# Another written order for the whole instruction list of a Mamba-2 and low-rank mixer kernel

## The chip, the cores and the metric

The kernel runs on one core of a Trainium2 chip. Its engines are TensorE (PE, the matrix products; PEld is its loading of weights), VectorE (DVE), ScalarE (ACT), GpSimd (POOL) and SyncE (SP, whose queue issues the DMAs). The metric is the time of one execution on the device in microseconds, the median of several runs. The profile is of one execution; its span is counted from the first to the last recorded instruction.

## The reference

The input is x (4 batches, 8 heads, 768 steps, 32 channels), a decay a for each step, and B and C (16 states a step). All is float32, though U, V, w_ch1 and w_ch2 come as float64 words.

```python
for c in range(nc):                          # chunks of 32 steps
    cum = np.cumsum(la, axis=-1)             # la = log(clip(a))
    M = einsum('bhin,bhjn->bhij', Cc, Bc) * exp(cum_i - cum_j) * causal
    y = einsum('bhij,bhjd->bhid', M, xc)                     # inside the chunk
    y += einsum('bhin,bhnd->bhid', Cc, state) * exp(cum)     # from before it
    state = decay_full * state + sum_j(Bc * xc * exp(cum_last - cum))
# y of all heads side by side: X of (4, 768, 256)
u = X + (X^T @ U @ V)^T                      # U: 768 x 32, V: 32 x 768
out = u + relu(u @ w_ch1) @ w_ch2            # 256 -> 1024 -> 256
```

## The kernel before

The first half (the scan) takes the steps in 12 **pairs** of two 128-step blocks, three pairs a batch: pairs 0 to 2 are batch 0, and so on. The second half (the mixer) takes each batch in two halves of 384 steps, with the 1024 inner channels in 8 groups.

**The order.** Nothing schedules these instructions: the text PLAN is a list of words, and `follow` (L886) goes through it and emits the instructions of each word, so each engine gets its instructions in the order of the words. An engine works its own list in order and waits at the first instruction that lacks its input. A shorter text, LOADS, is gone through before PLAN and issues the first loads. The words, with k a pair, b a batch, j a half and m an inner group:

- **F**n: the next bank of PSUM that is taken is first written by n products that nobody reads (`idle`, L139). The number is set, not added to (`fills[0] = n`), so a later F ahead of the bank replaces it.
- **A**i: the decays. A0 is product L370, A1 the products L374; each is followed by an exponential on ACT (L377). The logarithm is L342. K: what each state keeps.
- **Q**k.c, **P**k: prep, B and C times the decays (DVE, tile BC). **V**, **T**: turning, the transposes of BC on PE (w, x or y) and their copies T and Cm (by ACT, or Cm by DVE).
- **g**k: gram (L507), 16 products for C times B. **m**k, **M**k: the causal mask, two banks each (DVE, tile M). **s**k, **u**k: state (L542) and its update (L569: four on DVE, one on POOL).
- **n**k, **j**k: the two halves of the product inside the chunk (`intra`, L652); j has to follow one DVE instruction that comes after n's products, and where no such one is at hand it adds a copy to `settled`. **i**k: `inter` (L627). **y**k: the copy out to yT (ACT). **t**k, **O**k: transposes back to steps (`ytokens`, L679).
- **B**k, **X**k, **w**n: loads of B and C, of x, and of weight blocks (SP, `begin`, L195). Each of these words holds its first DMA until the last DVE instruction emitted so far is done. SP issues in order, so what stands behind a held DMA stands too. **L**k: B and C and x of pair k, held in the same way. V0 and U0 in LOADS are the loads of V and U, not held.
- **c**c: one of three steps of the conversion of weight block c from float64 words to float32 (`to_fp32`, L417 and L422): two instructions on DVE and one on ACT; one on DVE; the addition on POOL. Block 0 is U and V; 1 to 5 are w_ch1 (w1f); 6 to 9 are w_ch2.
- **v**0: spread, V copied to the form that the mixer needs (copy L838, products L844, copies to Vs). **R**c: a step of splitting a weight block in rounded parts.
- **p**b, **q**b, **a**b.j: X^T @ U (L705), its parts (L713), and the product with V that DVE adds to yT (L723). **S**b.j: the split of u in three parts (ACT L746, then DVE), in one buffer with w1f.
- **U**b.j.m: in batch 0, four products of 128x384 in plain float32 and a relu. **f**, **e**, **h** b.j.m: elsewhere, u @ w_ch1 in four and two products of rounded parts, the relu on ACT (L785) after e, and a difference on DVE in h. **d**b.j.k.n: piece n of the product with w_ch2 for 128 steps; the last piece is followed by the sum on DVE and the output's DMA. The products of U, f, e and d all have line L751.

Two banks of PSUM stand behind each of the tags w, x, z and y; a bank is taken again when its last reader is done.

Of the kernel before, what the change touches and what calls it, by code (L numbers as in the profile page):

```python
# [10 lines left out]
FP32 = mybir.dt.float32  # L11
INT32 = mybir.dt.int32
UINT32 = mybir.dt.uint32
FP32R = mybir.dt.float32r
WCOLS = 512
NWORDS = 15
# [14 lines left out]

LOADS = (
    'B0 X0 B1 V0 U0 X1 B2 X2 B3 ')
PLAN = (
# [36 lines left out]


@with_exitstack
def kernel(
# [28 lines left out]
    P = 128  # L105
    NB, NH, S, D = x.shape
    N = B.shape[-1]
    NC = S // P
    NPR = NC // 2
    DM = NH * D  # L110
    RK = moe_U.shape[1]
# [6 lines left out]
    NQ = NM // 2  # L118
# [75 lines left out]
    def begin(**kwargs):  # L194
        op = nc.sync.dma_start(**kwargs)  # L195
        if until:
            hold(op, until.pop())

    def load_bc(k, blocks=(0, 1)):
        b, q = pairs[k]  # L200
        if k not in bc_sb:
            bc_sb[k] = raw.tile([P, NH, 2, 2, N], FP32, tag="bc", name="bc")
        for c in blocks:
            begin(
                out=bc_sb[k][:, :, 0, c],
                in_=B[b, :, ts(2 * q + c, P), :].rearrange("h s n -> s h n"))
            if c == 0:
                begin(
                    out=bc_sb[k][:, :, 1].rearrange("p h t n -> p h (t n)"),
                    in_=C[b, :, ts(q, 2 * P), :].rearrange("h (p t) n -> p h (t n)", t=2))  # L210
# [17 lines left out]
    w1all = mix.tile([P, NQ, NCB, W], FP32, tag="u", name="w1f", bufs=1)  # L228
    w1f = [w1all[:, c] for c in range(NQ)]
    w2 = [const.tile([P, NM, DM], FP32R, name=f"w2{i}") for i in range(2)]  # L230
    weights = []
    w2f, w2b = {}, {}

    def w2c(n, dtype):
        return (w2f if dtype == FP32 else w2b).setdefault(n, mix.tile(
            [P, 2, DM], dtype, tag=f"w2c{n}", name=f"w2c{n}", bufs=1))


    def words_of(dst):
        p, i, j = dst.shape  # L240
        t = raw.tile([P, 2 * WCOLS], INT32, tag="words", name="words", bufs=NWORDS)
        weights.append((dst, t[:p, :2 * i * j]))
        return t[:p, :2 * i * j]

    def each(parts, *index):
        return [part[index] for part in parts]

    def load_words(dst, src):

        p, i, j = dst.shape  # L250
        t = words_of(dst)
        begin(out=t.rearrange("p (i j) -> p i j", i=i), in_=src)

    U2, V2, w12, w22 = (w.bitcast(INT32) for w in (moe_U, moe_V, moe_w_ch1, moe_w_ch2))
# [3 lines left out]
    own = {}  # L258

    def load_v():  # L260
        own["UV"] = words_of(UV)
        for q in range(4):
            begin(out=own["UV"][ts(q, Q), 2 * NC * RK:], in_=V2[:, ts(q, 2 * NC * RK)])

    def load_u():
        begin(out=own["UV"][:, :2 * NC * RK].rearrange("p (c r) -> p c r", c=NC),
                          in_=U2.rearrange("(c p) r -> p c r", p=P))

    def load_w(n):
        if n < 2:  # L270
            if n == 0:
                own["w"] = words_of(w1f[0])
                weights.pop()
            dst, t = w1f[0][:, :, ts(n, P)], own["w"][:, ts(n, 2 * NCB * P)]
            weights.append((dst, t))
            begin(out=t.rearrange("p (i j) -> p i j", i=NCB),
                  in_=w13[:, :, ts(n, 2 * P)])
        elif n <= NQ:
            load_words(w1f[n - 1], w13[:, :, ts(n - 1, 2 * quarter)])
        else:  # L280
            m = 2 * (n - NQ - 1)
            load_words(w2c(n - NQ - 1, FP32), w22[m * P:(m + 2) * P].rearrange(
                "(m p) d -> p m d", p=P))

    def load(k):
        if k < NB * NPR:
            load_bc(k)
            load_x(k)

    loads = dict(B=load_bc, X=load_x, w=load_w)  # L290
    for word in LOADS.split():
        dict(loads, V=lambda n: load_v(), U=lambda n: load_u())[word[0]](int(word[1:]))

    ident = const.tile([P, P], FP32)
    make_identity(nc, ident)
# [578 lines left out]
    def ytokens_of(k, v):  # L874
# [1 line left out]

    scans = dict(P=prep, T=turned, g=gram, s=state, m=lambda k: mask(k, (0, 1)),
                 M=lambda k: mask(k, (2, 3)), u=update, i=inter, n=lambda k: intra(k, 0),
                 j=crossed, y=yout, t=ytokens, L=load, Q=lambda k, c: prep(k, c, 1),
                 O=ytokens_of,  # L880
                 V=lambda k, c, v: turn(k, c, 1, "wx"[v // 2], vector if v % 2 else None))
    whole = dict(c=convert, R=refined, A=lambda i: decays(every_batch, "w", [i]),
# [3 lines left out]
    def follow(plan):  # L886

        for word in plan.split():
            name, at = word[0], [int(v) for v in word[1:].split(".")]
            if name in "BXwL":  # L890
                until[:] = [vector.last]
            if name in loads:
                loads[name](*at)
            elif name in scans:
                scans[name](*at)
            elif name in whole:
                whole[name](*at)
            else:
                b, *at = at
                if b not in mx:  # L900
                    mx[b] = mixer(b)
                getattr(mx[b], name)(*at)
            until.clear()
# [32 lines left out]
```

## Time and profile before

| | |
|---|---|
| Median of 3 runs | 230.32 us (230.38, 229.53, 230.32) |
| Profiled execution | 229.32 us |
| its span | 227.6 us |
| granted TensorE clock, mean | 0.992 |
| PE busy | 215.0 us |
| DVE busy | 146.5 us |
| ACT busy | 107.9 us |
| POOL busy | 33.9 us |
| DMA | 14.56 MB, mean 64 GB/s |

The page cuts the span into 40 slices of some 5.7 us. Each digit is the busy share of a slice in tenths (9 is 90% or more); PEclk is the clock that TensorE was granted, in tenths of full speed; DMA is the busy share of the DMA engines:

```profile
PE   7867979999999999999999999999999999999993
PEld 5644636666658889887999897698999999999993
DVE  4597867678632686479746546967746964945731
ACT  2334643756854366532456511465445654636410
POOL 3031232335075003015200010000000000000000
PEclk9999988999999999999999999999999999999999
DMA  6896878976560164211430001000010000000011
```

The chain that ended last is followed back from the last instruction; its shares by engine, then by line:

```profile
PE 82%; DVE 10%; issue 2%; ACT 2%; POOL 1%; POOLq 0%; DVEq 0%
PE x L751 29%; PE z L751 20%; PE y L751 12%; PE y L652 3%; PE y L627 3%; DVE M L169 3%; PE x L507 2%; PE w L679 2%; DVE words L169 2%; PE w L705 2%; DVE S L169 2%; PE w L475 2%; DVE BC L169 2%; PE w L542 1%; PE w L139 1%
```

All of DVE's instructions bear the line of the helper that records them, L169, so they are told apart by their tiles. A row of a timeline gives the start in us, the busy time, engine, line, operation, tiles, and the number of instructions drawn together; in square brackets stands how long the engine was idle before it, and what ended that.

### The profile page before, as it was taken

The numbers are of one execution on the slowest core, as the hardware profiler recorded it, in microseconds if no ns is written. First come the engines' busy times: TensorE is split into PE (matmuls) and PEld (weight loads), VectorE is DVE, ScalarE is ACT, GpSimd is POOL, SyncE is SP. The second block draws the span as 40 slices with busy tenths as digits, with TensorE's granted clock in tenths as the row PEclk, the third lists the DMA queues.
The fourth block names the chain that finished last, engine by engine and source line by source line (L and its number), as shares of the span: only waits on it lengthen the run. The fifth ranks groups of instructions, "written<-read, shape, count | busy, mean of one in ns | idle before, by whom it ended". The sixth has DMA issues, their size and how long they took to land.

```text
span 227.6 us, 6973 instructions
## 1 busy us (share of the span) xinstructions
PE 215.0 (94%) x3004; PEld 183.3 (81%) x3004; DVE 146.5 (64%) x312; ACT 107.9 (47%) x250; POOL 33.9 (15%) x43
## 2 busy tenths in 40 slices
PE   7867979999999999999999999999999999999993
PEld 5644636666658889887999897698999999999993
DVE  4597867678632686479746546967746964945731
ACT  2334643756854366532456511465445654636410
POOL 3031232335075003015200010000000000000000
PEclk9999988999999999999999999999999999999999
DMA  6896878976560164211430001000010000000011
GB/s 95 137 130 111 154 180 162 232 106 202 80 94 23 35 106 49 42 32 50 53 65 27 22 27 49 3 3 0 3 46 3 24 0 26 23 23 26 23 46 46
DMA packets 69518, 14.56 MB, mean 64 GB/s; under 512 B 63792, under 2 KB 67696, under 8 KB 69488
## 3 DMA queue, kind: packets, MB, share of 16 engines
q1 hardware_dynamic: 69488, 14.13, 31.5%
q8 instruction: 23, 0.38, 0.6%
q14 instruction: 7, 0.06, 0.1%
HBM read 10.98 MB, written 3.15 MB: 62 GB/s over the span
## 4 chain that ended last, share of the span: by engine, by line
PE 82%; DVE 10%; issue 2%; ACT 2%; POOL 1%; POOLq 0%; DVEq 0%
PE x L751 29%; PE z L751 20%; PE y L751 12%; PE y L652 3%; PE y L627 3%; DVE M L169 3%; PE x L507 2%; PE w L679 2%; DVE words L169 2%; PE w L705 2%; DVE S L169 2%; PE w L475 2%; DVE BC L169 2%; PE w L542 1%; PE w L139 1%
## 5 line engine op out<-in xcount | busy, mean ns | idle before, releaser
L751 PE MATMUL x<-u,w 128*128 128x384 f32 x144 | 33.3, 345 | 0.1
L751 PE MATMUL z<-u,w 128*128 128x384 f32 x144 | 33.0, 344 | 0.0
L169 DVE SCALAR_TENSOR_TENSOR words<-words 128x768 fp32r<-128x768 f32 (+3 forms) x34 | 29.7, 873 | 2.1 <-PE y L751 0.4
L751 PEld LDWEIGHTS x<-u,w 128*128 128x128 f32 x144 | 24.5, 188 | 1.1 <-ACT words L785 0.4
L751 PEld LDWEIGHTS z<-u,w 128*128 128x128 f32 x144 | 24.8, 188 | 0.3
L169 DVE SCALAR_TENSOR_TENSOR words<-x,words 128x384 fp32r<-128x384 f32 x24 | 13.2, 555 | 17.7 <-ACT words L785 17.5
L756 ACT ACTIVATE x<-x 128x384 f32<-128x384 f32 (+1 forms) x30 | 13.7, 455 | 21.8 <-PE x L751 19.6
L751 PE MATMUL x<-w2c,words 128*128 128x256 f32 x112 | 22.4, 338 | 0.0
L756 ACT ACTIVATE z<-z 128x384 f32<-128x384 f32 (+1 forms) x27 | 12.5, 464 | 15.3 <-PE z L751 14.4
L569 POOL TENSOR_TENSOR Sm<-S,own 128x256 f32<-128x256 f32 (+1 forms) x12 | 7.7, 640 | 78.6 <-DVE S L169 60.1
L751 PEld LDWEIGHTS x<-w2c,words 128*128 128x128 f32 x112 | 18.3, 189 | 1.4
L751 PE MATMUL y<-w,words 128*128 128x256 f32 x144 | 19.3, 282 | 0.0
L751 PEld LDWEIGHTS y<-w,words 128*128 128x128 f32 x144 | 18.6, 190 | 0.0
L169 DVE SCALAR_TENSOR_TENSOR words<-z,words 128x384 fp32r<-128x384 f32 x24 | 13.2, 552 | 2.6 <-ACT words L785 2.6
L785 ACT ACTIVATE words<-x 128x384 fp32r<-128x384 f32 x24 | 11.7, 493 | 6.8 <-PE x L751 6.8
L785 ACT ACTIVATE words<-z 128x384 fp32r<-128x384 f32 x24 | 11.7, 491 | 6.7 <-PE z L751 6.7
L169 DVE TENSOR_TENSOR BC<-bc,F 128x512 f32<-128x512 f32 (+2 forms) x18 | 10.4, 594 | 5.5 <-ACT F L377 2.8
L507 PE MATMUL x<-Cm,T 32*64 32x128 f32 x192 | 11.0, 306 | 2.5 <-issue 1.4
L652 PE MATMUL y<-M,x 64*32 64x64 f32 x768 | 12.0, 223 | 1.5 <-DVE settled L169 1.5
L751 PE MATMUL x<-w,words 128*128 128x256 f32 x96 | 13.4, 284 | 0.0
L652 PEld LDWEIGHTS y<-M,x 64*32 64x32 f32 x768 | 8.2, 105 | 6.0 <-DVE settled L169 2.7
L751 PEld LDWEIGHTS x<-w,words 128*128 128x128 f32 x96 | 12.6, 190 | 0.1
(148 smaller groups left out, 406.4 us busy)
## 6 DMA issues: line engine op xcount, KB each, us to landing
words<-in_moe_w_ch_dram SPq DMA_DIRECT2D x7, 512.0 KB, 5.6
x<-in_x_dram SPq DMA_DIRECT2D x24, 128.0 KB, 3.4
out_dram<-ytok SPq DMA_DIRECT2D x24, 128.0 KB, 1.7
bc<-in_B_dram SPq DMA_DIRECT2D x24, 64.0 KB, 3.0
bc<-in_C_dram SPq DMA_DIRECT2D x12, 128.0 KB, 3.1
words<-in_moe_w_ch_dram SPq DMA_DIRECT2D x2, 256.0 KB, 3.2
words<-in_moe_V_dram SPq DMA_DIRECT2D x4, 48.0 KB, 2.0
words<-in_moe_U_dram SPq DMA_DIRECT2D x1, 192.0 KB, 3.0
```

Of the source, the lines that this page charges most:

```text
L139: nc.tensor.matmul(out=t[:, :m * w].rearrange("p (m i) -> p m i", i=w), lhsT=ident, rhs=ident[:, None, :w].to_broadcast([P, m, w]), start= ...
L169: self.last = call(*args, **kwargs)
L475: nc.tensor.transpose(out=tp[:, i, v], in_=s["BC"][:, i, c + v].rearrange("p h n -> p (h n)"), identity=ident)
L507: nc.tensor.matmul(out=g[r][cols, c], lhsT=s["T"][rows, 0, c, cols], rhs=s["Cm"][rows, :, :, ts(2 * c + p, Q)].rearrange("r v t i -> r v i ...
L569: nc.gpsimd.tensor_tensor(out=s["Sm"][:, sl], in0=s["S"][:, sl].rearrange("p i (s d) -> p i s d", s=2), in1=own2[:, b, 4 * q + sl.start:4 ...
L627: behind["first"].append(nc.tensor.matmul(out=y[r // 2][ts(r % 2, H), c, p], lhsT=own[ts(r, Q)], rhs=s["T"][ts(r, Q), 1, :, ts(2 * c + p, ...
L652: product = nc.tensor.matmul(out=y[n][ts(i, Q), c, p], lhsT=x_sb[k][half, c, h], rhs=s["M"][half, h // 2, c, h % 2], start=fresh(k, n, [i] ...
L679: nc.tensor.transpose(out=t[:, c, g], in_=yT[b][:, g, ts(2 * q + c, P)], identity=ident)
L705: nc.tensor.matmul(out=p[ts(c % 4, Q)], lhsT=U_sb[:, c], rhs=ytok[b][:, c], start=c < 4, stop=True, skip_group_check=True)
L751: nc.tensor.matmul(out=t, lhsT=lhsT, rhs=rhs, start=start, stop=True, skip_group_check=True)
L756: nc.scalar.activation(t, t, AF.Copy, scale=1.0 + EPS)
L785: nc.scalar.activation(gs[j, m // 2][0][:, m % 2], t, AF.Relu, scale=NEAR)
```

## The change

The two texts LOADS and PLAN become one PLAN with another order. The operations are those of before, save the fills: three products (F2 and F1) in place of five F words whose numbers add up to 13. The first loads stand in the list as words with a Y ahead (YB0, YX0, YV0, YU0), and are not held. L words are gone; their loads are B and X words. Weight blocks are kept by number, so that they can be loaded in any order.

The beginning of the list, before and after:

```diff
-LOADS = (
-    'B0 X0 B1 V0 U0 X1 B2 X2 B3 ')
 PLAN = (
-    'F5 A0 Q0.0 F1 F2 F4 w0 Q0.1 A1 Q0.2 V0.0.0 Q1.0 V0.1.1 K0 s0 Q1.2 g0 m0 Q1.1 M0 V1.0.2 '
-    'V1.1.2 u0 n0 g1 c0 c0 c0 M1 F1 i0 Q2.0 s1 j0 y0 m1 Q2.2 Q2.1 V2.0.2 u1 V2.1.3 n1 i1 g2 j1 y1 '
-    'B5 s2 m2 M2 w1 v0 u2 O0.0 w2 w3 c1 c1 c1 i2 P3 n2 j2 y2 t1 X3 T3 T3 B4 c2 c2 P5 O2.1 p0 g3 '
-    'c3 c3 w4 w5 m3 q0 M3 T5 w6 T5 a0.1 a0.0 s3 X4 c4 c4 c2 P4 U0.1.0 c5 c3 U0.0.3 U0.0.0 U0.0.2 '
-    'c4 c5 B6 X5 U0.1.1 T4 T4 U0.0.4 u3 n3 c6 i3 R2 g4 s4 j3 R1 M4 R0 c5 X6 m4 u4 U0.0.7 P6 c6 '
+    'F2 YB0 A0 Q0.0 A1 F1 YB1 Q0.1 Q0.2 V0.0.0 Q1.0 V0.1.1 Q1.1 K0 Q1.2 g0 m0 YX0 s0 M0 V1.1.2 '
+    'V1.0.2 n0 YB2 g1 YX1 w0 u0 Q2.2 i0 Q2.1 Q2.0 V2.0.2 m1 s1 j0 y0 M1 u1 V2.1.3 c1 n1 i1 g2 YV0 '
+    'YU0 c0 YX2 w1 j1 s2 y1 YB3 c0 c0 B5 m2 M2 X3 v0 u2 c2 c2 c2 O0.0 t1 i2 w2 B4 n2 j2 y2 P3 T3 T3 '
+    'c1 c1 R0 O2.1 p0 g3 P5 m3 q0 M3 T5 T5 a0.1 w4 X4 n3 s3 u3 X5 w3 U0.1.1 w6 B6 c3 P4 a0.0 U0.1.0 '
+    'i3 w5 c3 c5 c5 w8 T4 T4 w7 U0.0.0 c3 R1 U0.0.1 U0.0.2 U0.1.3 B11 j3 g4 B10 s4 y3 c5 U0.1.2 m4 '
```

Some places further on that differ (the whole list of the third and the fourth batch's words is reordered in the same manner):

```diff
-    'e1.1.2 h1.1.2 T10 e1.1.3 f1.1.4 f1.1.5 n8 i8 s10 j8 e1.1.4 e1.1.5 y8 d1.1.0.0 h1.1.3 '
+    'n8 h1.1.6 s10 j8 y8 h1.1.7 f1.1.3 u10 f1.1.4 e1.1.2 f1.1.5 h1.1.2 t7 T9 e1.1.4 h1.1.4 e1.1.3 '
+    'h1.1.3 e1.1.5 T9 d1.1.0.0 T10 d1.1.2.0 d1.1.1.0 d1.1.2.1 d1.1.2.2 d1.1.1.1 d1.1.0.1 h1.1.5 '
...
-    't8 g9 m9 p2 T11 i9 M9 q2 T11 g10 m10 n9 M10 a2.0 s11 j9 u11 y9 g11 m11 S2.0 M11 i10 t9 n10 '
+    'd1.1.1.5 t8 g9 T11 m9 M9 T11 p2 g10 m10 q2 M10 i9 n9 a2.0 s11 j9 y9 g11 m11 S2.0 n10 i10 '
...
-    'd2.0.0.0 h2.0.7 d2.0.1.0 d2.0.1.1 y11 a2.1 S2.1 d2.0.0.1 d2.0.0.2 d2.0.0.3 d2.0.1.2 d2.0.1.3 '
-    't10 t11 d2.0.1.4 d2.0.1.5 d2.0.0.4 d2.0.0.5 f2.1.1 f2.1.0 f2.1.2 f2.1.3 e2.1.0 h2.1.0 e2.1.1 '
+    'e2.0.3 j11 d2.0.0.0 h2.0.2 h2.0.3 d2.0.0.1 d2.0.1.0 d2.0.1.1 d2.0.1.2 S2.1 f2.1.0 d2.0.1.3 '
+    'd2.0.0.2 d2.0.0.3 d2.0.1.4 d2.0.1.5 e2.1.0 d2.0.0.4 d2.0.0.5 f2.1.1 h2.1.0 d2.0.2.0 y11 '
...
-    'd2.1.0.0 h2.1.6 a3.1 d2.1.0.1 d2.1.0.2 d2.1.2.1 d2.1.2.2 S3.0 f3.0.2 f3.0.3 f3.0.4 h2.1.7 '
+    'e2.1.6 h2.1.6 e2.1.7 S3.0 h2.1.7 d2.1.2.0 d2.1.2.1 d2.1.2.2 d2.1.0.1 d2.1.0.2 f3.0.2 f3.0.3 '
```

And the code around it:

```diff
-    weights = []
+    weights = {}
...
+    def both_words():
+        return weights[0][1] if 0 in weights else words_of(0, UV)
...
-            load_words(w1f[n - 1], w13[:, :, ts(n - 1, 2 * quarter)])
+            load_words(n + 1, w1f[n - 1], w13[:, :, ts(n - 1, 2 * quarter)])
...
-    for word in LOADS.split():
-        dict(loads, V=lambda n: load_v(), U=lambda n: load_u())[word[0]](int(word[1:]))
+    early = dict(loads, V=lambda n: load_v(), U=lambda n: load_u())
...
-            name, at = word[0], [int(v) for v in word[1:].split(".")]
-            if name in "BXwL":
+            name, rest = (word[:2], word[2:]) if word[0] == "Y" else (word[0], word[1:])
+            at = [int(v) for v in rest.split(".")]
+            if name in "BXw":
                 until[:] = [vector.last]
-            if name in loads:
+            if name[0] == "Y":
+                early[name[1]](*at)
+            elif name in loads:
```

More of the change, by code (lines that the diff above doesn't have):

```diff
@@ L236, in w2c, with words_of @@
             [P, 2, DM], dtype, tag=f"w2c{n}", name=f"w2c{n}", bufs=1))
-    def words_of(dst):
+    def words_of(c, dst):
         p, i, j = dst.shape
         t = raw.tile([P, 2 * WCOLS], INT32, tag="words", name="words", bufs=NWORDS)
-        weights.append((dst, t[:p, :2 * i * j]))
+        weights[c] = dst, t[:p, :2 * i * j]
         return t[:p, :2 * i * j]
@@ L246, in each, with load_words @@
         return [part[index] for part in parts]
-    def load_words(dst, src):
+    def load_words(c, dst, src):
         p, i, j = dst.shape
-        t = words_of(dst)
+        t = words_of(c, dst)
         begin(out=t.rearrange("p (i j) -> p i j", i=i), in_=src)
@@ L260, in load_v @@
     def load_v():
-        own["UV"] = words_of(UV)
+        t = both_words()
         for q in range(4):
-            begin(out=own["UV"][ts(q, Q), 2 * NC * RK:], in_=V2[:, ts(q, 2 * NC * RK)])
+            begin(out=t[ts(q, Q), 2 * NC * RK:], in_=V2[:, ts(q, 2 * NC * RK)])
+    def both_words():
+        return weights[0][1] if 0 in weights else words_of(0, UV)
     def load_u():
-        begin(out=own["UV"][:, :2 * NC * RK].rearrange("p (c r) -> p c r", c=NC),
+        begin(out=both_words()[:, :2 * NC * RK].rearrange("p (c r) -> p c r", c=NC),
                           in_=U2.rearrange("(c p) r -> p c r", p=P))
@@ L270, in load_w @@
         if n < 2:
-            if n == 0:
-                own["w"] = words_of(w1f[0])
-                weights.pop()
+            if "w" not in own:
+                own["w"] = raw.tile([P, 2 * WCOLS], INT32, tag="words", name="words", bufs=NWORDS)
             dst, t = w1f[0][:, :, ts(n, P)], own["w"][:, ts(n, 2 * NCB * P)]
-            weights.append((dst, t))
+            weights[n + 1] = dst, t
             begin(out=t.rearrange("p (i j) -> p i j", i=NCB),
@@ L278, in load_w @@
         elif n <= NQ:
-            load_words(w1f[n - 1], w13[:, :, ts(n - 1, 2 * quarter)])
+            load_words(n + 1, w1f[n - 1], w13[:, :, ts(n - 1, 2 * quarter)])
         else:
             m = 2 * (n - NQ - 1)
-            load_words(w2c(n - NQ - 1, FP32), w22[m * P:(m + 2) * P].rearrange(
+            load_words(n + 1, w2c(n - NQ - 1, FP32), w22[m * P:(m + 2) * P].rearrange(
                 "(m p) d -> p m d", p=P))
[L285 to L288, printed above, removed]
     loads = dict(B=load_bc, X=load_x, w=load_w)
-    for word in LOADS.split():
-        dict(loads, V=lambda n: load_v(), U=lambda n: load_u())[word[0]](int(word[1:]))
+    early = dict(loads, V=lambda n: load_v(), U=lambda n: load_u())
     ident = const.tile([P, P], FP32)
@@ L878 @@
                  M=lambda k: mask(k, (2, 3)), u=update, i=inter, n=lambda k: intra(k, 0),
-                 j=crossed, y=yout, t=ytokens, L=load, Q=lambda k, c: prep(k, c, 1),
+                 j=crossed, y=yout, t=ytokens, Q=lambda k, c: prep(k, c, 1),
                  O=ytokens_of,
```

51 rows, old and new, of the table PLAN are left out of this document.

## The prediction

> **What bounds the kernel now.** I read the page first, then the busy time in stretches of 10 us, then the timelines of the first 40 us engine by engine, and last the stretches cut where the clock changes. From the page (span and busy sums):
>
> ```profile
> span 227.6 us, 6973 instructions
> ...
> PE 215.0 (94%) x3004; PEld 183.3 (81%) x3004; DVE 146.5 (64%) x312; ACT 107.9 (47%) x250; POOL 33.9 (15%) x43
> ```
>
> From the stretches (busy us and instructions of PE, PEld, DVE, ACT, POOL, then clock, DMA share, GB/s):
>
> ```profile
> 10.00:20.00 10.00, 7.07 (x266) 4.43 (x258) 9.50 (x29) 4.08 (x14) 2.35 (x4) 1.00 0.83 123
> 10.00:40.00 30.00, 24.21 (x620) 15.49 (x613) 23.95 (x66) 13.56 (x40) 7.55 (x9) 0.94 0.80 150
> 160.00:170.00 10.00, 10.00 (x77) 10.00 (x76) 6.25 (x11) 3.90 (x10) 0.00 (x0) 1.00 0.07 26
> ```
>
> TensorE (PE) is busy 94% of the span; at 160 us it works 10.00 of 10 us and VectorE (DVE) 6.25. Early it is otherwise: from 10 to 20 us DVE works 9.50 and PE 7.07, and from 10 to 40 us PE is idle for 30.00 - 24.21 = 5.8 us and the mean clock is 0.94. A new order leaves PE the same products apart from the fills. So it can win or lose two things: PE's idle and slow time before 40 us, and the small stalls after. The profiled execution took 229.32 us, 1.7 us around its span of 227.6; the three timed runs had a median of 230.32, 1.0 above it. The sum is made against 229.32. About 0.5% (1.15 us) is what a measurement of this kernel can tell from no change.
>
> **The head: fills and decays.** PE's timeline, then ACT's and DVE's:
>
> ```profile
> 3.77 2.10 PE L139 MATMUL w<-ident 128*128 128x128 f32 x10
> 5.70 0.49 PE L370 MATMUL w<-la,ref 128*128 128x192 f32 x2
> ...
> 7.01 0.57 PE L374 MATMUL w<-la,ref 128*64 128x96 f32 x8
> ```
>
> ```profile
> 4.07 0.36 ACT L342 ACTIVATE la<-la 128x192 f32<-128x192 f32 x1 [1.99 <-DVE la L169]
> ...
> 7.63 0.34 ACT L377 ACTIVATE F<-w 128x192 f32<-128x192 f32 x1 [1.06 <-PE w L374]
> ```
>
> ```profile
> 8.00 0.63 DVE L169 TENSOR_TENSOR BC<-bc,F 128x256 f32<-128x256 f32 x2 [0.90 <-ACT F L377]
> ...
> 12.28 0.75 DVE L169 TENSOR_TENSOR M<-z,causal 128x256 int32<-128x256 int32 x2
> ...
> 14.12 1.05 DVE L169 TENSOR_SCALAR words<-words 128x384 f32<-128x384 f32 x2
> 15.21 0.56 DVE L169 SCALAR_TENSOR_TENSOR words<-words 128x384 int32<-128x384 int32 x1
> ...
> 19.44 0.60 DVE L169 TENSOR_SCALAR Cm<-x,slot 128x128 f32<-128x128 f32 x2
> 20.99 0.15 DVE L169 COPY settled<-slot 128x1 f32<-128x1 f32 x1 [0.94 <-PE y L627]
> 21.55 0.76 DVE L169 TENSOR_TENSOR M<-x,causal 128x256 int32<-128x256 int32 x2 [0.41 <-PE z L507]
> ...
> 26.85 0.50 DVE L169 TENSOR_SCALAR words<-words 128x256 f32<-128x256 f32 x2 [0.56 <-DMA words<-in_moe_w_ch_dram]
> ```
>
> A word F sets one number, which the next bank uses; so "F1 F2 F4" gives 4 fills, and 5 + 4 + 1 = 10 products run now, two records each. In the new order 2 and 1 run. The logarithm is ready at 4.07 + 0.36 = 4.43, but L370 starts at 5.70, behind ten records of 0.21. Four records end at 3.77 + 0.84 = 4.61: 1.1 sooner. The second decay (A1) follows it at once, where now Q0.0 and four fills lie between; L374 moves from 7.01 to about 5.0, its exponential from 7.63 to 5.7, and DVE's prep at 8.00, which sat idle 0.90 for it, to 6.1. **Gain 1.9.** From there to the last mask of the first pair (12.28 + 0.75 = 13.03) DVE has the same work and is the bound, so the mask ends near 11.1. The fill that stays is a quarter us of PE ahead of a transpose that waits for DVE anyway.
>
> **Loads that move.** SP's timeline and the page's table of issues (last column: us to landing):
>
> ```profile
> 3.07 1.52 SPq L195 DMA_DIRECT2D x<-in_x_dram  x2
> ...
> 6.79 2.12 SPq L195 DMA_DIRECT2D words<-in_moe_V_dram  x4
> 8.95 0.42 SPq L195 DMA_DIRECT2D words<-in_moe_U_dram  x1
> ```
>
> ```profile
> words<-in_moe_w_ch_dram SPq DMA_DIRECT2D x7, 512.0 KB, 5.6
> x<-in_x_dram SPq DMA_DIRECT2D x24, 128.0 KB, 3.4
> ...
> words<-in_moe_U_dram SPq DMA_DIRECT2D x1, 192.0 KB, 3.0
> ```
>
> The second pair's B and C go ahead of the first x, so x is issued about 2.2 later (4.59, where its issue ends now, to 6.79, where V's begins, is theirs), near 5.3 to 6.8, and lands 3.4 on, at 8.7 to 10; its reader s0 now stands behind g0 (about 8.9) and DVE has masks until 11.1: cost 0, and 0.5 without that cover. V and U, issued from 6.79 to 9.37 now, stand behind the second x and w0, and w0 is held until the last mask (11.1). Behind it on SP queue V, U, the third x and later loads: V and U are issued from about 11.6 to 14.1, and U lands 3.0 on, at 17.1. Their conversion c0 (14.12 now) stands later as well: after the mask DVE has u0, three preps, four masks, u1 and two Cm, which now take from 13.03 to 19.44 + 0.60 = 20.04 with c0's 1.6 among them, so 5.4 without; with c1's first step (0.50 at 26.85) it is free at 17.0. So DVE waits 0 to 2.6 (landing as slow as the 5.6 of the large loads), I take 0.3, the end nearest to U's own row. c1's first step (0.5) comes in ahead of the spread. But c1 and c0 now fill the waits of 0.94 and 0.41 in which DVE stood for the products of the second pair: **gain 0.55** (1.35 - 0.5 - 0.3). V's spread, at 22.94, comes near 20.5.
>
> **From the spread to the first U.** PE's timeline, DVE's, and the stretches of the clock's changes:
>
> ```profile
> 22.94 0.35 PE L844 MATMUL y<-Vn,ident 32*32 32x192 f32 x2 [0.76 <-ACT Vn L838]
> ...
> 31.85 0.34 PE L507 MATMUL x<-Cm,T 32*64 32x128 f32 x1 [1.39 <-issue]
> ...
> 36.27 1.56 PE L751 MATMUL x<-yT,w1f 128*128 128x384 f32 x4
> ```
>
> ```profile
> 30.02 1.02 DVE L169 TENSOR_SCALAR words<-words 128x512 f32<-128x512 f32 x2 [0.95 <-DMA words<-in_moe_w_ch_dram]
> ...
> 31.69 0.42 DVE L169 TENSOR_TENSOR M<-x,causal 128x256 int32<-128x256 int32 x1
> 32.37 0.42 DVE L169 TENSOR_TENSOR M<-x,causal 128x256 int32<-128x256 int32 x1 [0.26 <-PE z L507]
> ```
>
> ```profile
> 19.10:22.50 3.40, 2.36 (x143) 1.73 (x120) 2.02 (x8) 1.22 (x5) 0.62 (x1) 1.00 0.56 110
> ...
> 29.36:32.78 3.42, 2.03 (x37) 1.12 (x35) 2.46 (x5) 1.19 (x3) 1.61 (x2) 1.00 0.77 182
> 32.78:36.19 3.41, 3.34 (x41) 2.20 (x39) 2.69 (x8) 2.27 (x5) 0.41 (x1) 0.50 0.64 80
> ```
>
> These 13.3 us hold three things. PE stands 1.39 in the middle of g3, for nothing that the profile shows. Then c3's conversion (0.95 of wait for w2, then 1.7 us) stands on DVE ahead of g3's mask at 31.69; it moves behind the first add to yT. The two overlap: the second mask waited for PE until 32.37. If the gap goes, c3 would be late next, and it is gone too. Whether the gap goes I can't tell: 0 to 1.39, taken 0.7, since in the new order one 512 KB load is in flight there instead of two. Last, the clock is half from 32.78 to 36.19, right after the stretch with the least PE work (2.03 of 3.42). Full clock would save up to half of 3.34, 1.7; I take 1.0, since DVE's adds to yT lie beside it. The two products of a0.0 leave this stretch and the 32 of n3 enter: even. **Gain 1.7**; the first U starts near 36.27 - 1.9 - 0.55 - 1.7 = 32.1.
>
> [...]
>
> ```profile
> q8 instruction: 23, 0.38, 0.6%
> ```
>
> **Behind the first U, and late.** From the chain of work, then the page's groups (mean ns) and PE's timeline:
>
> ```profile
> 63.93 1.29 PE z L751 x4
> ...
> 88.65 0.70 PE x L751 x4
> ...
> 214.65 9.56 PE y L751 x80
> ```
>
> ```profile
> L785 ACT ACTIVATE words<-x 128x384 fp32r<-128x384 f32 x24 | 11.7, 493 | 6.8 <-PE x L751 6.8
> ...
> L746 ACT ACTIVATE u<-yT 128x768 fp32r<-128x768 f32 x6 | 5.1, 847 | 5.1 <-DVE yT L169 5.1
> ```
>
> ```profile
> 104.90 0.34 PE L507 MATMUL x<-Cm,T 32*64 32x128 f32 x1 [0.45 <-DVE ytok L169]
> ```
>
> A U takes 1.29. U0.1.1, U0.1.0, U0.0.0 and U0.0.1 with a0.0, i3 and T4 between (1.5, by estimate) give PE work to 32.1 + 6.7 = 38.8. U0.0.2 then needs c3, whose first step comes after u3 near 34; two steps of DVE and one of GpSimd end it near 38: covered, by 0.7. w4 is held until the add to yT and lands 5.6 later, near 38; U0.1.7, its reader, is due at 44. Cost 0 each, 1 without cover. R0's first step stands on ACT ahead of the copy of p0, which waits for PE: 0.
>
> Late, some covers get thin. An f takes 0.70 and a piece of a d 0.48 (9.56 / 20). Four times (d1.1.0.0, d2.0.0.0, d2.1.2.1, d3.1.2.1) one piece or little more stands between an e and the reader of its relu (0.49 and some 0.2 of hand-over, by estimate from the starts of both rows): 0.2 each. S2.1 and S3.0 (0.85 on ACT, then a pass on DVE) stand closer to the first f, with one buffer for u: 0.3 each. The third batch's p, q and a stand closer: 0.1. **Loss 1.5**, bounds 0.5 to 2.5. On the other side the stall at 104.90 (0.45 of idle, and slow products around it) falls away, because its M and S order differs: **gain 0.7**, bounds 0 to 1.1. B8's load waits for P7's read, and X8, X7 and outputs queue behind it on SP; x of pair 7 is due some 25 us later: 0.
>
> **Sum.** 229.32 - 1.9 - 0.55 - 1.7 + 1.5 - 0.7 = 225.97. A timed median lay 1.0 above the profiled run before; one profiled run may be a low draw, so I add half: **226.5 us**.
>
> **The rivals.** The first ends slower: **the clock**. The one drop followed 3.4 us with 2.03 of PE work; the next lowest stretch, 2.36, kept it. In the new order the stretch near 8.9 to 12.3 us has no fills: s0, four transposes, n0 and most of g1, near 2.1 by the records' times, between the two. One closed window costs about 1 (half of some 2 us of products, partly hidden): 227.5, in the forecast's range. If it stays closed until the U's, six windows of about 2.4 busy us (the row at 19.10) become 6 x 4.8 = 28.8 in 20.5, so up to 8 more; a quarter of it under waits leaves 6: 232.5. It decides from the fourth closed window on, where it has cost the 3. [...]
>
> The second: **late weights**. If V and U land 5.6 after issue, c0 stalls 2.3 more, and the gap in g3 comes back (0.7): 229.5. For it: DMA share 0.83 in 10 to 20 us and all of it behind one held load.
>
> The third: the change **doesn't do what it says**. The fills ran in time that was idle, if the first loads and not the exponential set the prep's start; then 1.9 is not had: 228.4. Against it: the idle 0.90 at 8.00 is put to the exponential.
>
> **How the numbers follow.** Forecast 0.62 (own range 224.5 to 228.5: the bounds of gap, clock and late covers), late weights 0.15, clock 0.13, third 0.10. Low end 224.5 (gap and clock fully won); the high end reaches to 231.0, past late weights, and leaves out the clock. Faster by over 0.5% (under 229.2): 0.58 + 0.04 + 0.01 + 0.07 = 0.70; slower (over 231.5): 0.03 + 0.11 = 0.14; the rest 0.16.
>
> **What would show it.** Right: the second exponential near 5.7, the last mask of the first pair near 11, V's spread near 20.5 with little DVE idle before it, the first U near 32, no row of half clock beside it, and from 45 on PE as full as now with stalls below 0.5. Wrong: DVE idle on V's or U's DMA ahead of c0; a granted clock below 0.9 in any stretch from 5 to 30 us; PE waiting for GpSimd's w1f between U's; or PE's idle after 120 us up by over 2.

## The result, and the profile after

The changed kernel took 229.2 us (median of 20 runs) beside 230.2 of the kernel before (20 runs). The ratio is 0.9936, 95% interval 0.9914 to 0.9959, which is 1.5 us; the medians lie 1.0 apart, since medians count every execution and the ratios, here and below, leave out those more than 1.5% above the fastest of their kernel. The forecast was 226.5. So the sign was right and the size was not: 2.7 us of the forecast did not come.

The profile that belongs to this measurement is of an execution of 231.28 us with TensorE's clock at half for 10.24 us, so most lines below are from a second profile of the same kernel (the run after_again), of an execution of 229.18 us, close to its median of 229.17. In the new file the same lines stand a little lower in number (L167 for L169, L745 for L751). From that page (span, busy sums, clock in tenths over 40 slices):

```profile
span 227.5 us, 6951 instructions
...
PE 215.1 (95%) x2990; PEld 181.3 (80%) x2990; DVE 145.3 (64%) x313; ACT 108.4 (48%) x250; POOL 31.9 (14%) x43
...
PEclk9999799999999999999999999999999999999999
```

PE has 14 records fewer (the seven fills that went) and is as busy as before; the span is 227.5 where it was 227.6. The weak slice of the clock has moved from the sixth and seventh to the fifth one. **Where the time went** is best seen by cutting both traces at places where each has done the same work: the first product that uses V (word a0.1), the first of pair 7's intra part (n7), and the first of pair 8's ytokens (t8). Here are the stretches (PE's busy time and records come first) of the kernel before, then of the changed one:

```profile
0.00:33.96 33.96, 26.09 (x617) 18.00 (x617) 23.45 (x73) 14.63 (x41) 8.01 (x20) 0.98 0.78 135
33.96:103.59 69.63, 69.33 (x912) 52.80 (x912) 45.30 (x97) 38.15 (x82) 21.21 (x18) 0.98 0.50 95
103.59:138.14 34.55, 34.10 (x528) 32.37 (x528) 20.93 (x44) 14.44 (x34) 4.19 (x5) 1.00 0.19 40
138.14:227.60 89.46, 85.49 (x952) 80.14 (x950) 56.86 (x101) 40.73 (x93) 0.51 (x1) 1.00 0.06 22
```

```profile
0.00:32.26 32.26, 25.55 (x602) 16.97 (x603) 20.85 (x70) 15.29 (x42) 6.67 (x19) 0.95 0.76 125
32.26:103.80 71.54, 69.94 (x912) 52.48 (x912) 47.20 (x100) 37.78 (x82) 20.44 (x18) 1.00 0.55 104
103.80:136.93 33.13, 33.12 (x528) 32.01 (x528) 21.04 (x45) 14.05 (x34) 4.27 (x5) 1.00 0.13 34
136.93:227.50 90.57, 86.47 (x952) 79.84 (x950) 56.26 (x101) 41.26 (x94) 0.51 (x1) 1.00 0.06 22
```

The records agree (617 less 602 are fills and one product at the edge; then 912, 528 and 952 in both). The changed kernel gains 1.70, loses 1.91, gains 1.42 and loses 1.11: in sum 0.1. The forecast had -4.15 for the first (its sum up to the first U), 0, -0.5 and +1.3. The first U itself starts here:

```profile
33.90 1.56 PE L745 MATMUL z<-yT,w1f 128*128 128x384 f32 x4
```

It stood at 36.27 before, and the forecast had it at 32.1. By this cut 2.37 are gained up to the first U, and 2.58 are lost from there to n7 (69.90 beside 67.32).

DVE's rows of the head, and PE's first product of V's spread:

```profile
10.44 0.75 DVE L167 TENSOR_TENSOR M<-z,causal 128x256 int32<-128x256 int32 x2
...
13.84 0.49 DVE L167 TENSOR_TENSOR BC<-bc,F 128x128 f32<-128x128 f32 x2 [1.13 <-DMA bc<-in_B_dram]
...
19.03 0.63 DVE L167 TENSOR_SCALAR words<-words 128x384 f32<-128x384 f32 x2 [1.06 <-DMA words<-in_moe_U_dram]
```

```profile
21.84 0.35 PE L838 MATMUL y<-Vn,ident 32*32 32x192 f32 x2 [0.92 <-ACT Vn L832]
```

The last mask of the first pair ends at 11.19 (13.03 before): the head gained its 1.84. Then two waits that were not there stand on DVE: 1.13 for the B of pair 2, and 1.06 for U. The loads of pair 2's B and C are issued sooner than before (from 7.00 to 9.75, where it was 10.63 to 14.02), but their readers have moved further: the preps that stood at 16.35 and 17.71 now stand at 12.29 and 13.84, ahead of the second pair's masks. The spread starts 1.10 earlier, not 2.45. And in the second stretch stands one row that answers to the 1.39 in the middle of g3, from which PE is now free:

```profile
51.82 0.81 PE L745 MATMUL x<-yT,w1f 128*128 128x384 f32 x2
54.06 0.81 PE L745 MATMUL x<-yT,w1f 128*128 128x384 f32 x2 [1.43 <-issue]
```

PE has done two of the four products of one word (U0.0.4), and then stands 1.43 for "issue", that is, for nothing that the profile shows.

### The profile page after: what moved, and what is told of

It reads as the page before. It is cut to its first block, busy times and chain, and to the rows that moved or that the text cites. A ratio compares the mean times of both kernels' runs of the same rounds, so it can differ in the third digit from the quotient of the medians.

```text
span 229.6 us, 6951 instructions
## 1 busy us (share of the span) xinstructions
PE 217.4 (95%) x2990; PEld 183.0 (80%) x2990; DVE 145.5 (63%) x313; ACT 108.2 (47%) x250; POOL 31.8 (14%) x43
## 4 chain that ended last, share of the span: by engine, by line
PE 87%; DVE 5%; DMA 2%; issue 1%; SPq 1%; ACT 1%; POOL 1%; DVEq 0%; POOLq 0%
PE x L745 29%; PE z L745 22%; PE y L745 12%; PE y L646 3%; PE y L621 3%; PE w L469 2%; DVE words L167 2%; PE x L501 2%; PE w L699 2%; PE w L673 2%; DMA words<-in_moe_U_dram 2%; SPq L193 1%; PE w L536 1%; PE z L501 1%; DVE M L167 1%
## 5 line engine op out<-in xcount | busy, mean ns | idle before, releaser
L745 PE MATMUL x<-u,w 128*128 128x384 f32 x144 | 33.1, 346 | 0.1
L745 PE MATMUL z<-u,w 128*128 128x384 f32 x144 | 32.3, 343 | 0.1
L167 DVE SCALAR_TENSOR_TENSOR words<-words 128x768 fp32r<-128x768 f32 (+3 forms) x34 | 29.2, 859 | 3.0 <-PE y L745 1.8
L745 PEld LDWEIGHTS z<-u,w 128*128 128x128 f32 x144 | 24.8, 188 | 1.2 <-issue 0.4
L745 PEld LDWEIGHTS x<-u,w 128*128 128x128 f32 x144 | 24.0, 188 | 1.2 <-DVE u L167 0.4
L745 PE MATMUL x<-w2c,words 128*128 128x256 f32 x112 | 22.5, 339 | 0.0
L563 POOL TENSOR_TENSOR Sm<-S,own 128x256 f32<-128x256 f32 (+1 forms) x12 | 7.7, 641 | 90.0 <-DVE S L167 54.9
L745 PE MATMUL y<-w,words 128*128 128x256 f32 x144 | 20.0, 284 | 0.0
L167 DVE SCALAR_TENSOR_TENSOR words<-x,words 128x384 fp32r<-128x384 f32 x24 | 13.2, 552 | 10.4 <-ACT words L779 10.4
L745 PEld LDWEIGHTS x<-w2c,words 128*128 128x128 f32 x112 | 18.1, 189 | 1.8 <-issue 0.4
L745 PEld LDWEIGHTS y<-w,words 128*128 128x128 f32 x144 | 19.1, 190 | 0.1
L167 DVE SCALAR_TENSOR_TENSOR words<-z,words 128x384 fp32r<-128x384 f32 x24 | 13.2, 549 | 4.6 <-ACT words L779 4.5
L745 PE MATMUL x<-yT,w1f 128*128 128x384 f32 x32 | 11.9, 490 | 2.0 <-issue 1.9
L646 PE MATMUL y<-M,x 64*32 64x64 f32 x768 | 12.3, 230 | 1.5 <-DVE settled L167 1.4
L745 PE MATMUL x<-w,words 128*128 128x256 f32 x96 | 13.6, 286 | 0.0
L167 DVE TENSOR_TENSOR M<-x,causal 128x256 int32<-128x256 int32 x24 | 9.0, 417 | 7.1 <-PE z L501 7.1
L745 PEld LDWEIGHTS x<-w,words 128*128 128x128 f32 x96 | 12.3, 191 | 0.2
```

Source lines behind the costliest of these rows:

```text
L167: self.last = call(*args, **kwargs)
L563: nc.gpsimd.tensor_tensor(out=s["Sm"][:, sl], in0=s["S"][:, sl].rearrange("p i (s d) -> p i s d", s=2), in1=own2[:, b, 4 * q + sl.start:4 ...
L646: product = nc.tensor.matmul(out=y[n][ts(i, Q), c, p], lhsT=x_sb[k][half, c, h], rhs=s["M"][half, h // 2, c, h % 2], start=fresh(k, n, [i] ...
L745: nc.tensor.matmul(out=t, lhsT=lhsT, rhs=rhs, start=start, stop=True, skip_group_check=True)
```

## The experiments

**Theory A (the clock)**: the stretch near 18 to 22 us, in which PE waits for V, lets the clock go to half, and that is what was lost. **Theory B (late weights)**: the wait for U is. **Theory C**: TensorE waits for its own next block of instructions, in g3 before and in the U's now. Theory C', put up later, names the transfers that this block is late behind. The kernel before was run beside each (median 230.0 to 230.4):

| run | median us (runs) | ratio to before, 95% |
|---|---|---|
| uv_early | 229.83 (12) | 0.9973, 0.9941 to 1.0004 |
| fill_thin | 232.66 (6) | no interval |
| head_alone | 228.96 (12) | 0.9947, 0.9922 to 0.9972 |
| late_of_before | 228.32 (11) | 0.9907, 0.9879 to 0.9935 |
| after_again | 229.17 (12) | 0.9956, 0.9926 to 0.9986 |
| loads_later | 228.94 (12) | 0.9963, 0.9932 to 0.9994 |
| both_parts | 227.95 (12) | 0.9930, 0.9895 to 0.9965 |
| before_load_later | 230.48 (12) | 1.0038, 1.0004 to 1.0073 |
| weights_later | 231.38 (12) | 0.9999, 0.9962 to 1.0036 |
| all_later | 227.53 (6) | 0.9876, 0.9851 to 0.9902 |
| all_later_late | 225.96 (5) | 0.9807, 0.9779 to 0.9835 |
| all_later_fills | 228.34 (6) | 0.9894, 0.9860 to 0.9928 |
| all_later_uv | 227.56 (6) | 0.9891, 0.9868 to 0.9915 |
| all_later_late_uv | 226.71 (6) | 0.9852, 0.9827 to 0.9877 |

### uv_early: the loads of V and U ahead of w0

```diff
-YX1 w0 u0
+YX1 YV0 YU0 w0 u0
-c1 n1 i1 g2 YV0 YU0 c0 YX2
+n1 i1 g2 c0 YX2
-T3 T3 c1 c1 R0
+T3 T3 c1 c1 c1 R0
```

> The changed kernel with the loads of V and U issued before the first weight block, and the first step of block 1's conversion put behind block 0's. Theory A (the clock): the wait of 1.69 us for U goes, V's spread starts near 20.5 in place of 22.04, the stretch from 17.6 to 21 gets denser, and fewer executions fall to half clock: median 227.0 to 227.8. Theory B (late weights alone): the same 1.5 us come off in every execution and the clock is as low as before the edit (mean 0.985): 227.7. If the wait cost nothing: 229.2.

A miss for both theories: 229.83, not below the changed kernel. DVE's rows of its profile:

```profile
18.34 0.63 DVE L167 TENSOR_SCALAR words<-words 128x384 f32<-128x384 f32 x2 [1.63 <-issue]
...
21.12 0.36 DVE L167 TENSOR_TENSOR UV<-UV,Vn 128x192 f32<-128x192 f32 x1 [0.23 <-ACT Vn L832]
```

```profile
18.31 0.57 ACT L411 ACTIVATE words<-words 128x384 int32<-128x384 uint32 x1 [1.14 <-DMA words<-in_moe_U_dram]
```

DVE stands 1.63 there all the same, now for "issue". The row of ACT is of the same conversion, starts at the same time and is put down to U's load: it was issued at 14.59 (15.41 in after_again), since V's four issues ahead of it took 3.39 here, and landed 3.6 later. So DVE's wait too is most likely still the one for U, which the edit brought only some 0.8 forward. The spread comes 0.7 earlier than in after_again, and the standstill among the U's is 1.63. This run alone could not tell the wait's price (see all_later_uv).

### fill_thin: fills where PE waits

```diff
-j1 s2 y1
+j1 F3 s2 y1
```

> The changed kernel with three fills (1.3 us of TensorE) ahead of the state of pair 2, in the thin stretch near 20 us where TensorE waits for V. Theory A (the clock): the granted clock stays at 0.99 or above in most executions and the median falls from 229.2 to about 227.6, though nothing is done earlier. Theory B (late weights alone): no gain, 229.2 or up to 1.0 more for the fills.

Neither: it is 3.5 us slower in the median (five of its six executions took 231.3 to 233.9, one 227.9). The rows are of the one that took 233.89. PE's rows, and the stretches of its clock:

```profile
50.33 0.59 PE L745 MATMUL z<-yT,w1f 128*128 128x384 f32 x1
54.78 2.29 PE L745 MATMUL z<-yT,w1f 128*128 128x384 f32 x3 [3.86 <-issue]
```

```profile
52.53:59.36 6.83, 4.58 (x7) 2.53 (x8) 4.80 (x12) 1.03 (x3) 0.56 (x1) 0.50 0.84 102
```

The standstill is 3.86 here (50.92 to 54.78), and from 52.53 on the clock is at half for 6.83 us, in the U's, where PE is busy for all of the 4.58 from 54.78 to 59.36. For this execution that is the loss, by estimate: against after_again it is 4.7, the standstill is 2.43 longer, and half of the 4.58 of products at half clock is 2.3 (the product of U0.0.3 ahead of the standstill takes 0.59, the next one, at half clock, 1.01). The place is telling too: it is now between the first and the second product of U0.0.3, five records earlier than the two products of U0.0.4 where it stood. The three fills are six records more ahead of it. **So the place goes with the number of records ahead of it**, not with the work. The counts bear it out. In the profiles of the changed kernel, loads_later, weights_later, uv_early and both_parts 984 of PE's records start ahead of the standstill, in the two with fills 985, and in the kernel before 604. Theory C takes the packets of the queue "q8 instruction" (23, 0.38 MB, so some 16.5 KB each) for TensorE's instructions; the page does not say whose they are. The counts fit: the two places lie 380 records and three of these packets apart (the fourth packet of 23 starts ahead of the one, the seventh ahead of the other), which is 127 records a packet, and 23 times 127 is 2921 of PE's 2990 records. The clock went to half at 21.81 in this profile in spite of the fills.

### head_alone: the kernel before with the new head

```diff
-F5 A0 Q0.0 F1 F2 F4 w0 Q0.1 A1 Q0.2
+F2 A0 Q0.0 A1 F1 w0 Q0.1 Q0.2
-M1 F1 i0
+M1 i0
```

> The kernel before with the new head alone: two fills instead of ten, and the second decay behind the first. Forecast's step: exponential 1.2 to 1.9 earlier, median 230.2 - 1.5 = 228.7. Rival (the head's time is eaten by later waits or by the clock): within 0.5 of 230.2, or slower if the clock closes more often.

228.96: the forecast's step holds in the median (1.4 of 1.5), and the rival by which the fills ran in time that was idle is wrong. The clock is a little lower, though: 0.977 in the median of its executions beside 0.98 of the kernel before, and at half for 13.65 us in its profile, from 17.21 on.

### late_of_before: the order of before from t8 on

```diff
 ... d1.1.0.5 d1.1.1.5
-t8 g9 T11 m9 M9 T11 p2 ...     (the changed list)
+t8 g9 m9 p2 T11 i9 M9 ...      (the list before, to its end)
```

> The changed kernel up to the ytokens of pair 8 (near 139 us), the order of before from there. In the two traces the part behind this point takes 87.0 (changed) and 85.7 us (before). If the thin covers cost what the forecast said (1.5): 229.2 - 1.3 = 227.9. If that difference is noise: 229.2.

Faster than after_again by 0.85 in the median. The stretch from t8 to the end in its profile:

```profile
135.99:225.50 89.51, 85.66 (x952) 80.26 (x950) 56.66 (x101) 41.06 (x94) 0.51 (x1) 1.00 0.06 22
```

With 89.46 before, 90.57 in the changed kernel (90.59 in its other profile): the new order from t8 on costs 1.1, and that is no noise. That it is the thin covers is not shown: the waits that the profiles list for PE there sum to 0.6 in after_again and 0.7 before, and most of the loss stands in the busy time of the same 952 records (86.47 beside 85.49).

### after_again and loads_later: is it the transfers?

after_again is the changed kernel itself. loads_later:

```diff
-U0.1.3 B11 j3 g4 B10 s4 ... m4 B7 M4 ... P6 B9 R1 ... X6 c7 U0.0.7
+U0.1.3 j3 g4 s4 ... m4 M4 ... P6 R1 ... X6 c7 B11 B10 B7 B9 U0.0.7
```

> The changed kernel once more, for a second profile of it beside the next one on the same chip. Theory C (a late block of instructions): TensorE stands again between the second and the third product of U0.0.4, near 54 us, for 1 to 4 us, with an instruction packet that starts less than 1 us before; median near 229. Theory A (the thin stretch at 18 to 21 us): the row of half clock begins near 21 us, and the standstill at 54 us may be short.

> The changed kernel with the loads of B and C of pairs 11, 10, 7 and 9 (1 MB in small packets, issued from 41 to 57 us) moved behind the load of x of pair 6, some 8 us later; no engine's instructions change but SP's. Theory C: the standstill of 1.9 us near 54 goes, and with it the half clock that a long one brings: median 226.5 to 227.5, spread under 2 us. Theory A: the standstill may go, but the executions still differ with the clock of 18 to 31 us: median 228, spread as now (227 to 233).

after_again does as theory C says (above). loads_later is a miss for it: 228.94, and the standstill stays. PE's rows; the share of the DMA engines, in tenths, over 40 slices from 51.0 to 55.5; and the instruction packets (count, MB, share) that started in the 0.2 us from 52.4 on:

```profile
52.18 0.81 PE L745 MATMUL x<-yT,w1f 128*128 128x384 f32 x2
54.90 0.48 PE L745 MATMUL x<-yT,w1f 128*128 128x384 f32 x1 [1.91 <-issue]
```

```profile
DMA  9999998998953700000000000000000000000000
...
q8 instruction: 1, 0.02, 30.1%
```

An instruction packet starts at 52.4 to 52.6, as the other transfers end (the 14th slice, 52.6), and PE resumes at 54.90, with no transfer beside it. It is so in the others: in the kernel before a packet starts at 29.5 to 29.7 and PE resumes at 31.85 in g3; in the changed one at 53.6 to 53.8, and PE at 56.12; in after_again at 51.7 to 51.9, and PE at 54.06; in fill_thin at 52.2 to 52.4, and PE at 54.78. **From the packet to PE it is 2.2 to 2.6 us each time.** If this wait is for the packet, as theory C has it, the packet is late, and small loads of B and C are not what it is late behind; three loads of 512 KB (w5, w8, w7) are issued at 45.7.

### both_parts and before_load_later

both_parts is loads_later up to t8, with before's order from there. before_load_later:

```diff
-O0.0 w2 w3 c1
+O0.0 w2 c1
-p0 g3 c3
+p0 g3 w3 c3
```

> The changed kernel up to pair 8's ytokens with the later loads of the run loads_later, and the order of before from there. If the two edits add up: the gain of loads_later and 1 to 1.3 more; by theory C 225.5 to 226.5, by theory A 227 to 227.5.

> The kernel before with the load of weight block 3 (512 KB) moved behind the gram of pair 3, so that one such load fewer is in flight near 30 us, where TensorE stood 1.39 in the middle of that gram. Theory C: that standstill goes or falls under 0.5, median 230.3 - 1 to 1.5 = 229; if the standstill is no matter of the load: it stays, 230.3.

both_parts shows the late gain again (227.95, 1.0 below loads_later), with the standstill still 1.80. In before_load_later g3 runs through without a standstill, as theory C had it. But DVE waits 2.77 for a weight block in this profile, the clock is at half for 13.65 us, and the median is no better, so the price of that standstill is not settled. Why before keeps its time without its standstill stays open.

### weights_later, all_later, all_later_late

```diff
-c5 c5 w8 T4 T4 w7 U0.0.0
+c5 c5 T4 T4 U0.0.0
-U0.0.3 y4 u5 U0.0.4
+U0.0.3 y4 u5 w8 w7 U0.0.4
```

This is weights_later; all_later adds the edit of loads_later, and all_later_late has the order of before from t8 on as well.

> The changed kernel with the loads of weight blocks 8 and 7 (512 KB each, issued near 46 us with block 5) moved some 8 us later, behind the copy out of pair 5 and its state update; the loads of B and C stay. Theory C': the instruction packet of TensorE started late near 52 to 53.7 us because it stood behind these three large loads, and TensorE resumes some 2.3 us after it starts; with one load in place of three it starts before it is needed and the standstill of U0.0.4 goes: median 229.2 - 1.5 to 2 = 227.2 to 227.7. If the loads have nothing to do with it: 229.2, standstill as before.

> Both edits: the loads of weight blocks 8 and 7, and those of B and C of pairs 11, 10, 7 and 9, moved later, so that few transfers are in flight from 49 to 54 us. Theory C': no standstill near 54 us, 227.2 to 227.7. If the standstill stays here too, it is not the transfers of this stretch: 229.

> As all_later, with the order of before from pair 8's ytokens on. If the three edits add up: 229.2 - 1.7 - 1.3 = 226.2; without the gain of the standstill: 227.9.

weights_later missed, and shows why: PE's rows and a row of DVE.

```profile
52.49 0.81 PE L745 MATMUL x<-yT,w1f 128*128 128x384 f32 x2 [0.73 <-issue]
...
64.53 0.68 PE L646 MATMUL y<-M,x 64*32 64x64 f32 x32 [2.37 <-DVE settled L167]
```

```profile
63.05 0.77 DVE L167 TENSOR_SCALAR words<-words 128x512 f32<-128x512 f32 x2 [8.14 <-DMA words<-in_moe_w_ch_dram]
```

The standstill shrinks to 0.73. But SP issues the late weights at 58.2, behind the loads of B and C that are still queued; DVE waits for them 8.14, the `settled` copy stands behind it, and PE waits 2.37 for that copy. **The load that was moved took its reader's queue with it.** In all_later the B and C loads are out of the way, the weights go at 45.6 to 54.9, and the products of U0.0.4 read:

```profile
51.81 1.45 PE L745 MATMUL x<-yT,w1f 128*128 128x384 f32 x4
```

```profile
q8 instruction: 1, 0.02, 29.5%
```

Four products without a break. The packet starts in the 0.2 us from 50.1, while PE comes to that product near 52.4: 2.3 later, within the 2.2 to 2.6 of the others. The stretches around it, of all_later and then of after_again, both from the same word (U0.1.7) to U0.0.5 and on to n7:

```profile
46.68:53.10 6.42, 6.42 (x165) 4.15 (x164) 5.83 (x14) 3.23 (x8) 3.16 (x3) 1.00 0.32 89
53.10:102.17 49.07, 48.99 (x530) 39.48 (x528) 32.15 (x64) 27.06 (x59) 13.98 (x12) 1.00 0.50 88
```

```profile
46.68:54.70 8.02, 6.59 (x165) 4.14 (x164) 7.36 (x18) 3.62 (x8) 3.73 (x4) 1.00 0.94 239
54.70:103.80 49.10, 49.02 (x529) 39.44 (x527) 29.58 (x60) 26.76 (x57) 13.42 (x11) 1.00 0.38 60
```

The two kernels are level to 0.01 up to 46.68, then 1.60 apart, and stay so to the end; the medians lie 1.64 apart (229.17 and 227.53, beside 230.15 and 230.22 of the kernel before). With before's late order on top it is 225.96, as forecast for it (226.2): 1.9% faster than the kernel before, the best version here. Its stretch from t8 on takes 89.43 (from 135.37 to 224.80).

### all_later_fills: theory A once more

```diff
-j1 s2 y1
+j1 F3 s2 y1
```

> As all_later, with three fills ahead of the state of pair 2. Theory A, now without a standstill behind it: the clock is granted in full in more executions than in all_later (0.99 in the mean), and the median lies 0.5 to 1.5 below that of all_later. If the half clock of 18 to 26 us costs nothing, or the fills do not hold it up: the same as all_later or up to 1 more.

A miss: 228.34. The standstill is back with the shifted stream,

```profile
51.45 1.24 PE L745 MATMUL z<-yT,w1f 128*128 128x384 f32 x3 [1.37 <-issue]
```

and the clock goes to half at 20.20 all the same. These fills are no remedy. What half clock costs can be read better from three executions of one list, weights_later, after_again and the changed kernel's first profile, which do the same up to the first U. From the spread to a0.1 (the clock is the third number from the end):

```profile
21.50:30.92 9.42, 7.91 (x194) 5.02 (x195) 6.09 (x17) 5.92 (x16) 1.99 (x3) 1.00 0.81 130
```

```profile
21.84:32.26 10.42, 9.38 (x194) 6.04 (x195) 5.95 (x17) 6.01 (x16) 1.98 (x3) 0.84 0.84 136
```

```profile
22.04:33.88 11.84, 11.04 (x194) 7.29 (x195) 5.95 (x17) 6.00 (x16) 1.98 (x3) 0.61 0.81 131
```

194 records each: 9.42 at full clock, 10.42 with 3.41 us at half clock, 11.84 with 9.26 us (of the 10.24 in that execution the first 0.98 lie ahead of the spread). **A microsecond at half clock cost 0.26 to 0.29 here, a window of 3.41 some 0.9 to 1.0.**

### all_later_uv and all_later_late_uv: the wait for U

```diff
-YX1 w0 u0
+YX1 YV0 YU0 w0 u0
-c1 n1 i1 g2 YV0 YU0 c0 YX2
+n1 i1 g2 c0 YX2
-v0 u2 c2 c2 c2
+v0 u2 c1 c2 c2 c2
```

> As all_later, with the loads of V and U ahead of the first weight block, and the first step of block 1's conversion behind the update of pair 2. Theory (late weights): VectorE no longer waits 1.1 to 1.7 us for U, V's spread starts near 20.5, the first U near 33 in place of 33.9, and with no standstill behind it the gain reaches the end: median 227.5 - 0.9 = 226.6. Rival: the wait is hidden by what comes behind it (the conversions and weights of block 1 are then late): 227.5.

> As all_later_late, with the same two edits. By the theory 226.0 - 0.9 = 225.1; if the wait is hidden: 226.0.

The rival is right: 227.56 beside 227.53, and 226.71 beside 225.96. In the first one's profile c0 starts at 17.05 without a wait,

```profile
17.05 0.74 DVE L167 TENSOR_SCALAR words<-words 128x384 f32<-128x384 f32 x2
...
21.35 0.36 DVE L167 TENSOR_TENSOR UV<-UV,Vn 128x192 f32<-128x192 f32 x1 [0.98 <-ACT Vn L832]
```

and the spread comes only 0.4 sooner than in all_later, since one half of g2 stands 0.88 for "issue" ahead of the mask:

```profile
19.43 0.48 PE L501 MATMUL z<-Cm,T 32*64 32x128 f32 x2 [0.88 <-issue]
```

This is a standstill of the same kind. An instruction packet starts at 17.0 to 17.2, 2.3 earlier, and 350 records start ahead of it, which is two packets of 127 ahead of the 604. So with U out of the way PE's next wait was, by theory C, for a block of instructions. The wait for U is real on DVE, and taking it away was worth nothing measurable at the end.

## Why the prediction was wrong, point by point

- **Fills and decays, gain 1.9: right.** The mask of the first pair ended 1.84 earlier, and head_alone brought 1.4 in the median.
- **Loads that move, gain 0.55: wrong, it was a loss of 0.74.** From the mask to the spread it takes 10.65, before 9.91. The forecast counted U's wait at 0.3 (1.06 here, 1.69 in the other profile): it had U issued by 14.1, and U went at 15.41, behind 1.56 for the issue of w0 and 1.85 for V's. And it counted pair 2's preps without a wait for their B, which they now reach too early (1.13). By all_later_uv the part of it that U stands for is not what the end lacks.
- **From the spread to the first U, gain 1.7: half right.** To the first U it was 1.27 (12.06 beside 13.33), to a0.1 0.60. With the clock in full (weights_later) it is 9.42 where before took 33.96 - 22.94 = 11.02: 1.60. The gap in g3 did go, and c3's conversion with it; the clock did not stay. The forecast let the half clock go away with the thin stretch ahead of it, and found the thinnest new stretch at 8.9 to 12.3; it was at 19.1 to 22.5, where PE waits for V. The price that it gave one closed window (1.0) was right.
- **Whether the gap goes: the step that failed.** It was taken as 0.7 gained, the author's estimate, for one large load fewer in flight near g3. It went from g3, and one came back 380 records, or three packets, further down the stream, behind three large loads that the forecast had not looked at for this: 1.43 in after_again, 1.88 in the other profile, 0.73 to 3.86 in others. all_later, which moves only loads, wins 1.60 by its going. So the U's cost 1.91 (71.54 - 69.63), where the forecast had 0, and by all_later 1.60 of it goes with this standstill.
- **Late: loss 1.5, gain 0.7: the size of the loss right, the gain too small.** From t8 on 1.1 was lost (late_of_before, all_later_late), where the forecast had 1.3 of its 1.5; that its cause is the thin covers is not shown; the stretch n7 to t8 gained 1.42.
- **From profile to median.** Half of 1.0 was added for a low draw. By profile the change is worth 0.1, by median 1.0, so before's profile was a low draw by nearly all of it. The clock fits this: 0.992 in that profile, and 0.975 to 0.982 in the median of the executions of the kernel before that ran beside the experiments.

The sum of it against the forecast's 3.35: first stretch 2.45 short, U's 1.91 short, n7 to t8 0.9 over, late 0.2 over. Of the rivals, the clock was right in that a thin stretch was followed by half clock, and in its price, but not in its place, nor in its bar (see the last section). Late weights was right in its wait and not in its effect; the third, that the fills cost nothing, was wrong.

## What to carry to other kernels

A standstill for "issue" that the profile ties to nothing should be looked for in the stream of instructions before it is booked as won: see whether an instruction packet starts ahead of its end (here by 2.2 to 3.0 us), and what large loads are in flight there. Here it did not go with a new order, another came 380 records later; it was gone where two large loads and those of B and C were issued later (a DMA share of 0.32 beside 0.94 in the stretch ahead, all_later and after_again), and with three fills more it was back for 1.37. And when a load is moved, follow its reader and all that is queued behind that reader, as weights_later did not.

## What the runs showed of the hardware

- **Instruction packets.** After a standstill for "issue" PE resumes 2.2 to 3.0 us after a packet of some 16.5 KB starts (eight profiles; 2.65 to 2.85 in all_later_fills, 2.8 to 3.0 at a shorter standstill, 0.58 up to 19.02, in the changed kernel's first profile), whether or not other transfers run in that time: in loads_later they were through just after it started. By that what a standstill lasts is how late the packet starts. With two large loads moved later, and those of B and C, the packet started at 50.1 and there was no standstill (all_later); whether it had waited behind them or was asked for late is not shown. The page counts 23 packets, and in both profiles of the changed kernel as it was PE stood in this way behind at least one, for 1.43 and 1.88 us, and for 3.86 in fill_thin.
- **The clock.** PE's busy time in a stretch does not tell whether half clock follows. Here are two successive stretches of weights_later, then two of all_later_fills:

```profile
20.14:23.56 3.42, 2.15 (x55) 1.35 (x50) 3.08 (x11) 1.87 (x8) 1.44 (x2) 1.00 0.60 120
23.56:26.97 3.41, 2.39 (x104) 1.94 (x104) 1.49 (x4) 2.09 (x6) 1.27 (x2) 1.00 0.84 103
```

```profile
16.79:20.20 3.41, 2.36 (x97) 1.57 (x90) 1.99 (x8) 1.28 (x4) 0.30 (x1) 1.00 0.47 74
20.20:23.62 3.42, 3.42 (x66) 2.43 (x66) 2.98 (x10) 1.53 (x6) 1.51 (x2) 0.50 0.64 129
```

2.15 kept the clock; 2.36 lost it. In after_again the stretch ahead of the half clock had 1.76:

```profile
19.12:22.53 3.41, 1.76 (x89) 1.08 (x88) 3.14 (x11) 1.43 (x4) 1.01 (x1) 1.00 0.57 125
```

The bar that the forecast put between 2.03 and 2.36 does not hold, and what decides instead is not shown.
- **A standstill and half clock together**: in the profile of fill_thin the clock went to half at 52.53, within the standstill of 3.86 us that ended at 54.78, and stayed there for 6.83 us.
